# Reading the early pages' token lists ahead of the last scatters, with one flag and one branch at the end

## The chip, the cores and the metric

The kernel runs on one NeuronCore of a Trainium2 chip. The metric is the device time of one execution in microseconds (us), the median over several runs. The engines are named as in the profile: PE is TensorE (matrix products), DVE is VectorE, ACT is ScalarE, POOL is GpSimd, SP is SyncE, which here only issues DMA transfers and reads registers. The time before is 1185.52 us, the median of 3 runs (1181.2 to 1187.52).

## The reference

Three steps in float32, each on the output of the one before. The activations are 3072 tokens of 512 values in the second and third.

```python
# 1. banded attention, q, k, v: 4 x 8 x 768 x 64, window 128, 4 sinks
keep = (pos < n_sink) | ((rel >= 0) & (rel < window))
a = softmax(where(keep, scale * q @ k.T, -1e9))
x = (a @ v)                              # -> 3072 x 512
# 2. first MLP, 512 -> 2048 -> 512
h = x @ w_in;  x = (h - tanh(h)) @ w_out
# 3. routed MLP, 8 experts, top 1, 512 -> 1024 -> 512
logits = x @ w_gate + modality_bias[modality_id]
e_idx = argmax(logits);  probs = softmax(logits)
for e in range(8):
    mask = e_idx == e
    out[mask] = probs[mask, e] * (relu(x[mask] @ w1[e]) @ w2[e])
```

## The kernel before

**Chunks.** The tokens go through attention and the first MLP in 12 chunks of 256. The MLP of a chunk makes `h` (L175), three elementwise operations on DVE (`h` L189, `gy` L191) and ACT and POOL (`g`, L208 and L213), and the second product into `acc` (L245). Names carry the chunk: `gy11_4` belongs to chunk 11, the last. The chunk's result is stored in DRAM (`x2d`, L560), its router logits are computed (`lg`, L575), and `r_route` finds for each token its expert and its slot `sl` in a list of pages (L645). Two indirect scatters on POOL (L653) then write gate and token number to these slots in the DRAM tensor `xs`.

**Pages.** The slots are grouped into pages of 256, each of one expert. `r_order` puts the pages in the order in which they are computed, in the small tile `order`. Pages 0, 1 and 2 (`EARLY`) are chosen after chunk 10 among those that no token of chunk 11 can enter; the others are ordered after chunk 11 (names `ol...`). 13 pages are always computed (`NSTAT`); pages 13 to 18 stand in nested branches on the number of pages `npg` (L910 reads it, L915 branches), and behind them a branch on `redo` (L940, L941) leads to a general path for other masks. Neither is entered with these inputs.

**One page, and its names.** SP reads the expert from `order` (L718) and loads eight weight tiles `mr` of 512 KB each (L723). ACT casts each to `mh` (L731), DVE makes the remainder `ml` (L732): the split. SP reads the page number (L737) and loads the page's list `mpl` from `xs` (L740, 2 KB). DVE turns it into `mi` (L742) and `ms` (L744), and POOL gathers the rows of `x2d` by `ms` into two tiles `mx` (L750). PE transposes them (`mT`, L761), ACT and DVE make `mxt` (L764, L765). For each of 8 slices PE computes `mh` (12 matmuls, L775), ACT and DVE make `mg` (L778, L779), and PE adds six matmuls to `macc` (L792). At the end ACT scales by the gate (`mo`, L800) and POOL scatters the rows to `out` (L801). `mpl3` is page 3's list, `mg1_2` page 1's third slice.

**What sets the order.** Each step is filed with a time, as `add(time, function, ...)`; `emit` sorts by time and calls the functions, and a scheduler then orders each engine's queue within that. An engine takes its instructions strictly in that order: an instruction that waits holds all behind it. `m_events` files a page's steps; for the early pages no step comes before `first`, the time behind the early `r_order`. Weight tiles live in a pool of 33 buffers, gathered rows, page outputs and chunk outputs in a pool of 4, lists and their conversions in pools of 3.

Of the kernel before, what the change touches and what calls it, by code (L numbers as in the profile page):

```python
# [10 lines left out]
I32 = mybir.dt.int32  # L11
U8 = mybir.dt.uint8
AF = mybir.ActivationFunctionType
ALU = mybir.AluOpType
PSUM = bass.MemoryType.PSUM

P = 128
# [10 lines left out]
PG = 256  # L28
NPG = NT // PG + NE - 1
PADID = 4096.0  # L30
EARLY = 3
NSTAT = NT // PG + 1
# [8 lines left out]
class Kern:  # L41
# [658 lines left out]
    def r_redo(self, ok):  # L700

        nc = self.nc
        cp = self.cp
        mx, bad = cp.tile([P, 1], F32, name="ovmx"), cp.tile([P, 1], BF16, name="ovbad")
        nc.vector.tensor_reduce(out=mx, in_=self.over, axis=mybir.AxisListType.X, op=ALU.max)
        nc.vector.tensor_scalar(out=bad, in0=mx, scalar1=0.0, scalar2=None, op0=ALU.is_gt)
        ps = self.ps("x", F32, "ovps")
        nc.tensor.matmul(ps[:, :1], self.ones, bad, start=True, stop=True)
        t = cp.tile([P, 1], F32, name="ovt")
        nc.vector.tensor_scalar(out=t, in0=ps[:, :1], scalar1=0.0, scalar2=None, op0=ALU.is_equal)  # L710
        redo = cp.tile([P, 1], I32, name="redo")
        nc.vector.tensor_mul(t, t, ok)
        nc.vector.tensor_scalar(out=redo, in0=t, scalar1=-1.0, scalar2=1.0, op0=ALU.mult, op1=ALU.add)
        self.redo = redo


    def m_expert(self, g):
# [14 lines left out]
        nc.vector.tensor_sub(lo, r, f32(hi))  # L732
        self.mw[g, f] = (hi, lo)

    def m_xload(self, g):
        nc = self.nc
        pg = nc.sync.value_load(self.order[0:1, 0, g:g + 1], min_val=0, max_val=NPG - 1)  # L737
        n = PG // P
        pl = self.rp.tile([P, n, 2], F32, tag="mpl", name=f"mpl{g}", bufs=3)
        nc.sync.dma_start(pl, self.xs[bass.ds(pg * PG, PG), :].rearrange("(t p) w -> p t w", p=P))  # L740
        idx = self.rp.tile([P, n], I32, tag="mi", name=f"mi{g}", bufs=3)
        nc.vector.tensor_copy(idx, pl[:, :, 1])  # L742
        src = self.rp.tile([P, n], I32, tag="ms", name=f"ms{g}", bufs=3)
        nc.vector.scalar_tensor_tensor(out=src, in0=pl[:, :, 1], scalar=float(NT), in1=pl[:, :, 1],  # L744
                                       op0=ALU.is_lt, op1=ALU.mult)
        self.mx[g] = []
        rows = NT - CH if g < EARLY else NT
        for t in range(n):
            x = self.x2p.tile([P, DM], F32, tag="x2", name=f"mx{g}_{t}")
            nc.gpsimd.indirect_dma_start(out=x, out_offset=None, in_=self.x2d[:rows, :],  # L750
                                         in_offset=bass.IndirectOffsetOnAxis(ap=src[:, t:t + 1], axis=0))
            self.mx[g].append((x, idx[:, t:t + 1], pl[:, t, 0:1]))
# [54 lines left out]
    def m_events(self, add, g, t, t0=-1e9):  # L807
        n8 = FF // P
        o = self.o
        at = lambda d, fn, *a: add(max(t + d, t0), fn, *a)  # L810
        at(-o["me"], self.m_expert, g)
        at(-(o["mxe"] if g == 1 else o["mxl"]), self.m_xload, g)
        for j in range(PG // P):
            at(-o["mxt"] + 0.5 * j, self.m_xT, g, j)
            at(n8 + o["mlag"] - 0.5, self.m_out, g, j)
        for f in range(n8):
            at(f - o["mwl"], self.m_wload, g, f)
            at(f - o["mws"], self.m_wsplit, g, f)
            at(f, self.m_L1, g, f)
            at(f + o["mlag"], self.m_L2, g, f)  # L820
# [7 lines left out]
    def run_chunks(self, banded):  # L828
# [3 lines left out]
        with ExitStack() as st:  # L832
            pool = lambda n, b, **k: st.enter_context(tc.tile_pool(name=n, bufs=b, **k))
            self.yp = pool("y", self.o.get("y",2))
            self.xtp = pool("xt", self.o["bxt"])
            self.xpp = pool("xp", 1)
            if banded:
                self.rawp = pool("raw", self.o["raw"])
                self.spp = pool("sp", self.o["sp"])
                self.smp = pool("sm", self.o["bs"])  # L840
            self.gp = pool("g", self.o["bg"])
            self.psr = pool("psr", 6, space=PSUM)
            self.psa = pool("psa", 1, space=PSUM)
            self.x2p = pool("x2", self.o["x2"])
            self.rp = pool("rp", 1)
            self.X = None
            if banded:
                xs = pool("X", 1)
                self.X = xs.tile([P, 8, P], F32R, name="X")
                self.sT = [xs.tile([P, CH], F32R, name=f"sT{i}") for i in range(2)]  # L850
                for t in self.sT:
                    nc.gpsimd.memset(f32(t[2 * SK:]), 0.0)
            ev = []

            def add(t, fn, *a):
                ev.append((t, len(ev), fn, a))

            if banded:
                add(self.o["trc"], self.r_consts)
                add(self.o["trc"], self.r_reset)  # L860
            else:
                self.r_reset()
            add(self.o["tpf"], self.x_prefill, banded)
            for c in range(0 if banded else nch):
                add(16.0 * c - 2, self.x_load, c)
            for U in range(8 * nch if banded else 0):
                o = self.o
                t = 2.0 * U + o["u0"]
                add(t + o["tl"], self.a_load, U)
                add(t + o["tv"], self.a_loadv, U)  # L870
                if U >= o["nf"]:
                    add(t + o["ts"], self.a_split, U)
                    add(t + o["tsv"], self.a_splitv, U)
                for q in range(2):
                    add(t + o["tS"] + o["dS"] * q, self.a_S, U, q)
                    add(t + o["tN"] + o["dN"] * q, self.a_norm, U, q)
                    add(t + o["tT"] + o["dT"] * q, self.a_T, U, q)
                add(t + o["tPV"], self.a_PV, U)
            for f in range(NF):
                o = self.o  # L880
                add(f * o["wls"] + o["wl"], self.w_load, f, "i")
                add(f * o["wls"] + o["wl"] + o["wo"], self.w_load, f, "o")
                add(f * o["wds"] + o["wd"], self.w_decode, f, "i")
                add(f * o["wds"] + o["wd"] + o["wo"], self.w_decode, f, "o")
            for c in range(nch):
                t = 16.0 * c
                for pr in range(4):
                    add(t + self.o['txs'], self.xsplit, c, pr)
                for f in range(NF):
                    add(t + f, self.L1, c, f)  # L890
                    if f % 2:
                        add(t + f + self.o['tg'], self.gact if banded else self.gact_any, c, f // 2)
                    add(t + f + self.o["lag"], self.L2, c, f)
                t2 = t + NF - 0.9 + self.o["lag"]
                for q in range(CH // P):
                    add(t2 + self.o["tre"], self.r_evac, c, q)
                    add(t2 + self.o['trl'], self.r_logits, c, q)
                add(t2 + self.o['trr'], self.r_route, c)
                if c == nch - 2:
                    add(t2 + self.o["trr"] + .3, self.r_order, False)  # L900
                    first = t2 + self.o["trr"] + .35
            add(t2 + self.o["trr"] + .3, self.r_order, True)
            if banded:
                add(t2 + self.o["trr"] + .6, self.r_redo, self.ok)
            self.eg, self.mw, self.mx, self.mxt, self.mg, self.macc = {}, {}, {}, {}, {}, {}
            for g in range(NSTAT):
                self.m_events(add, g, 16.0 * nch + self.o["mt0"] + FF // P * g,
                              first if g < EARLY else t2 + self.o["trr"] + .35)
            self.emit(ev)
            np_ = nc.values_load(self.npi[0:1, 0:1], min_val=0, max_val=NPG)  # L910

            def rest(g):
                if g == NPG:
                    return
                with tc.If(np_ > g):  # L915
                    ev.clear()
                    self.m_events(add, g, 0.0)
                    self.emit(ev)
                    rest(g + 1)

            rest(NSTAT)

def program(tc, a, o={}):
    nc = tc.nc
    K = Kern(tc, a)
    K.o.update(o)
    with ExitStack() as st:
# [9 lines left out]
            K.ok = K.scalars(cp)  # L937
            K.band_masks(cp, sp)
        K.run_chunks(True)
        redo = nc.values_load(K.redo[0:1, 0:1], min_val=0, max_val=1)  # L940
        with tc.If(redo == 1):  # L941
            K.general()
            K.run_chunks(False)


def layouts(inp):
# [55 lines left out]
```

## Time and profile before

| | |
|---|---|
| median of 3 runs (lowest, highest) | 1185.52 us (1181.2, 1187.52) |
| the profiled execution: time, span | 1184.34 us, 1182.6 us |
| PE busy | 1118.5 us, 95% of the span, 7171 matmuls |
| DVE, ACT, POOL busy | 860.0, 689.8, 636.3 us |
| mean granted clock of PE | 0.98 |

The table by stretches says when an engine worked; `PEclk` in it is the clock granted to PE, 1.00 being full speed. In a timeline row the first number is the start and the second how long the instruction (or, with xN, the group) took; the bracket is the idle time of the engine before it and what ended that. What POOL does at the end in its sequencer (loads of flags, branches, semaphores, the drain) is in no busy time; the rows by source line list it, `POOLq` being POOL's sequencer.

### The profile page before, as it was taken

What the parts mean: (1) busy time and instruction counts of PE and PEld (TensorE: products, weight loads), DVE (VectorE), ACT (ScalarE), POOL (GpSimd) and SP (SyncE); (2) the same over time, 40 slices, a digit from 0 to 9 for tenths busy, and PEclk for the clock granted to TensorE, in tenths of its full rate; (3) what the DMA queues carried; (4) which work ended last, traced back from release to release, by engine and by line L of the source; (5) the groups of instructions that cost most, each with busy time, mean ns of one, the idle gap of its engine ahead of it and who ended that gap; (6) DMA issues with size and microseconds to landing.
All of it is one profiled execution on the core that took longest, in us unless ns stands there. A gap on an engine that the chain in (4) does not pass through costs nothing. (4 is left out here: it accounts for less than half of the span.)

```text
span 1182.6 us, 22303 instructions
## 1 busy us (share of the span) xinstructions
PE 1118.5 (95%) x7171; PEld 984.5 (83%) x7171; DVE 860.0 (73%) x2227; ACT 689.8 (58%) x1643; POOL 636.3 (54%) x877
## 2 busy tenths in 40 slices
PE   7889989999999999999999999999889999999992
PEld 3346789998999999998999998998778899999992
DVE  6989878787887878797878888756757565666610
ACT  3345565766666666666776757654536555556620
POOL 4887766767676767676776767643223112111200
PEclk9989999999999999999999999999989999999997
DMA  6654222313132222222222322003629776777500
GB/s 203 211 181 145 69 71 61 91 50 98 55 83 61 66 81 68 86 63 74 68 86 62 92 52 85 27 24 107 267 79 353 219 221 220 243 215 215 162 18 6
DMA packets 75127, 137.14 MB, mean 116 GB/s; under 512 B 16241, under 2 KB 51313, under 8 KB 74993
## 3 DMA queue, kind: packets, MB, share of 16 engines
q1 hardware_dynamic: 70064, 122.40, 34.0%
q0 software_dynamic: 4928, 13.14, 3.1%
q8 instruction: 61, 1.00, 0.4%
q14 instruction: 74, 0.60, 0.2%
HBM read 122.86 MB, written 13.17 MB: 115 GB/s over the span
## 5 line engine op out<-in xcount | busy, mean ns | idle before, releaser
L175 PE MATMUL h<-xt,wi 128*128 128x256 f32 x2304 | 350.6, 291 | 6.0 <-DVE xt L210 3.0
L175 PEld LDWEIGHTS h<-xt,wi 128*128 128x128 f32 x2304 | 313.1, 193 | 30.1 <-DVE xt L210 5.8
L245 PE MATMUL acc<-wo,g 128*128 128x512 f32 x1152 | 313.6, 399 | 5.1 <-POOL g L213 3.5
L245 PEld LDWEIGHTS acc<-wo,g 128*128 128x128 f32 x1152 | 201.8, 189 | 38.2 <-POOL g L213 5.4
L732 DVE TENSOR_TENSOR ml<-mr,mh 128x1024 fp32r<-128x1024 f32 x104 | 129.8, 1257 | 52.8 <-ACT mh L731 51.0
L213 POOL TENSOR_TENSOR g<-gy,g 128x512 fp32r<-128x512 f32 x96 | 132.4, 1379 | 63.0 <-ACT g L208 60.3
L775 PE MATMUL mh<-mxt,mh 128*128 128x256 f32 x832 | 156.1, 284 | 0.9 <-ACT mxt L764 0.7
L792 PE MATMUL macc<-mh,mg 128*128 128x512 f32 x416 | 147.9, 401 | 4.4 <-DVE mg L779 4.3
L775 PEld LDWEIGHTS mh<-mxt,mh 128*128 128x128 f32 x832 | 136.9, 192 | 9.4 <-ACT mxt L764 0.9
L801 POOL DMA_INDIRECT out_dram<-mo,mi x26 | 29.3, 1128 | 196.7 <-ACT mo L800 192.5
L352 POOL TENSOR_SCALAR_AFFINE_SELECT X<-fl 128x512 fp32r<-128x512 f32 (+1 forms) x192 | 117.0, 633 | 30.7 <-DVE fl L382 22.0
L325 ACT ACTIVATE e<-e,nm 128x160 f32<-128x160 f32 x192 | 81.8, 426 | 87.6 <-DVE nm L323 71.1
L731 ACT CAST mh<-mr 128x1024 fp32r<-128x1024 f32 x104 | 108.2, 1051 | 38.6 <-PE macc L792 25.3
L775 PE MATMUL mh<-mxt,ml 128*128 128x256 f32 x416 | 117.6, 284 | 0.0
L190 ACT ACTIVATE u<-u,kt 128x512 f32<-128x512 f32 x96 | 69.5, 723 | 44.5 <-DVE h L189 23.3
L334 POOL TENSOR_SCALAR e<-e,sm 128x160 f32<-128x160 f32 x192 | 88.5, 472 | 9.7 <-DVE sm L329 8.0
L792 PEld LDWEIGHTS macc<-mh,mg 128*128 128x128 f32 x416 | 77.9, 190 | 18.1 <-DVE mg L779 5.3
L778 ACT ACTIVATE mg<-mh 128x256 fp32r<-128x256 f32 x104 | 40.1, 386 | 90.0 <-PE mh L775 85.9
L213 POOL TENSOR_TENSOR B<-q,A 128x256 fp32r<-128x256 f32 x82 | 71.5, 871 | 39.1 <-ACT A L208 38.2
L213 DVE TENSOR_TENSOR K<-k,K 64x448 fp32r<-64x448 f32 x82 | 85.1, 1038 | 2.7
L213 POOL TENSOR_TENSOR V<-v,V 128x256 fp32r<-128x256 f32 x82 | 65.0, 793 | 35.3 <-ACT V L208 35.2
L792 PE MATMUL macc<-ml,mg 128*128 128x512 f32 x208 | 82.4, 396 | 0.0
(211 smaller groups left out, 2200.2 us busy)
## 6 DMA issues: line engine op xcount, KB each, us to landing
mr<-in_moe_w_dram SPq DMA_DIRECT2D x104, 512.0 KB
k<-in_k_dram SPq DMA_DIRECT2D x82, 224.0 KB
v<-in_v_dram SPq DMA_DIRECT2D x96, 128.0 KB
q<-in_q_dram SPq DMA_DIRECT2D x82, 128.0 KB
rawi<-in_moe_w_in_dram SPq DMA_DIRECT2D x16, 512.0 KB
rawo<-in_moe_w_out_dram SPq DMA_DIRECT2D x16, 512.0 KB
x2d<-x SPq DMA_DIRECT2D x24, 256.0 KB
k<-in_k_dram SPq DMA_DIRECT2D x14, 112.0 KB
```

Source lines behind the costliest of these rows:

```text
L175: nc.tensor.matmul(h, w[:, wl, k * P:(k + 1) * P], x[:, xl, k], start=(n == 0), stop=(n == 11))
L190: nc.scalar.activation(u, u, AF.Relu, bias=self.kt, accum_out=self.over[:, n:n + 1])
L213: (self.nc.vector if eng == "v" else self.nc.gpsimd).tensor_tensor(out=out, in0=a, in1=b, op=ALU.subtract)
L245: nc.tensor.matmul(o, g[:, gl, q:q + P], w[:, wl], start=(f == 0 and n == 0), stop=(f == NF - 1 and n == 2))
L325: nc.scalar.activation(e, e, AF.Exp, bias=nm, scale=-1.0, accum_out=u["sm"][:, t:t + 1])
L334: self.nc.gpsimd.tensor_scalar(out=e, in0=e, scalar1=r, scalar2=1.0, op0=ALU.mult, op1=ALU.mult)
L352: self.nc.gpsimd.affine_select(out=out, in_=in_, pattern=[[0, n], [s, P]], base=0, channel_multiplier=-s, compare_op=ALU.is_gt if prev els ...
L731: nc.scalar.copy(hi, r)
L732: nc.vector.tensor_sub(lo, r, f32(hi))
L775: nc.tensor.matmul(h, w[:, k * P:(k + 1) * P], x[:, xl, k], start=(n == 0), stop=(n == 11))
L778: nc.scalar.activation(gt[:, 0], h, AF.Relu)
L792: nc.tensor.matmul(self.macc[g][t], gt[:, gl, t * P:(t + 1) * P], w[:, DM:], start=(f == 0 and n == 0), stop=(f == n8 - 1 and n == 2))
```

## The change

`m_xload` is cut in two. `m_list` reads the page number, loads the list and makes `mi` and `ms`; `m_xload` issues the gathers. For pages 0, 1 and 2 `m_list` is filed at `first`, so that all three lists are read there; for the others it is filed just ahead of the gathers, as before. `r_redo` has two more DVE operations on 128x1 tiles for a flag `more`, 0 where there are at most 13 pages and no general path is needed. The code of pages 13 to 18 moves into a function of its own. At the end there is one load and one branch on `more`; inside it stand the pages beyond 13 and the branch on `redo`. Line numbers grow by 3 from L718 on and by 8 from L750 on; the end of the program moves from L998 to L1028.

```diff
@@ -712,6 +712,9 @@
         nc.vector.tensor_mul(t, t, ok)
         nc.vector.tensor_scalar(out=redo, in0=t, scalar1=-1.0, scalar2=1.0, op0=ALU.mult, op1=ALU.add)
         self.redo = redo
+        nc.vector.scalar_tensor_tensor(out=t, in0=self.npg, scalar=float(NSTAT), in1=t, op0=ALU.is_le, op1=ALU.mult)
+        self.more = cp.tile([P, 1], I32, name="more")
+        nc.vector.tensor_scalar(out=self.more, in0=t, scalar1=-1.0, scalar2=1.0, op0=ALU.mult, op1=ALU.add)
 
 
     def m_expert(self, g):
@@ -732,7 +735,7 @@
         nc.vector.tensor_sub(lo, r, f32(hi))
         self.mw[g, f] = (hi, lo)
 
-    def m_xload(self, g):
+    def m_list(self, g):
         nc = self.nc
         pg = nc.sync.value_load(self.order[0:1, 0, g:g + 1], min_val=0, max_val=NPG - 1)
         n = PG // P
@@ -743,9 +746,14 @@
         src = self.rp.tile([P, n], I32, tag="ms", name=f"ms{g}", bufs=3)
         nc.vector.scalar_tensor_tensor(out=src, in0=pl[:, :, 1], scalar=float(NT), in1=pl[:, :, 1],
                                        op0=ALU.is_lt, op1=ALU.mult)
+        self.ml[g] = (pl, idx, src)
+
+    def m_xload(self, g):
+        nc = self.nc
+        pl, idx, src = self.ml[g]
         self.mx[g] = []
         rows = NT - CH if g < EARLY else NT
-        for t in range(n):
+        for t in range(PG // P):
             x = self.x2p.tile([P, DM], F32, tag="x2", name=f"mx{g}_{t}")
             nc.gpsimd.indirect_dma_start(out=x, out_offset=None, in_=self.x2d[:rows, :],
                                          in_offset=bass.IndirectOffsetOnAxis(ap=src[:, t:t + 1], axis=0))
@@ -809,7 +817,12 @@
         o = self.o
         at = lambda d, fn, *a: add(max(t + d, t0), fn, *a)
         at(-o["me"], self.m_expert, g)
-        at(-(o["mxe"] if g == 1 else o["mxl"]), self.m_xload, g)
+        x0 = o["mxe"] if g == 1 else o["mxl"]
+        if g < EARLY and t0 > 0:
+            add(t0, self.m_list, g)
+        else:
+            at(-x0 - .01, self.m_list, g)
+        at(-x0, self.m_xload, g)
         for j in range(PG // P):
             at(-o["mxt"] + 0.5 * j, self.m_xT, g, j)
             at(n8 + o["mlag"] - 0.5, self.m_out, g, j)
@@ -902,23 +915,36 @@
             add(t2 + self.o["trr"] + .3, self.r_order, True)
             if banded:
                 add(t2 + self.o["trr"] + .6, self.r_redo, self.ok)
-            self.eg, self.mw, self.mx, self.mxt, self.mg, self.macc = {}, {}, {}, {}, {}, {}
+            self.eg, self.ml, self.mw, self.mx, self.mxt, self.mg, self.macc = {}, {}, {}, {}, {}, {}, {}
             for g in range(NSTAT):
                 self.m_events(add, g, 16.0 * nch + self.o["mt0"] + FF // P * g,
                               first if g < EARLY else t2 + self.o["trr"] + .35)
             self.emit(ev)
+
+    def more_pages(self):
+
+        tc, nc = self.tc, self.nc
+        with ExitStack() as st:
+            pool = lambda n, b, **k: st.enter_context(tc.tile_pool(name=n, bufs=b, **k))
+            self.xtp = pool("xt", self.o["bxt"])
+            self.gp = pool("g", self.o["bg"])
+            self.psr = pool("psr", 6, space=PSUM)
+            self.psa = pool("psa", 1, space=PSUM)
+            self.x2p = pool("x2", self.o["x2"])
+            self.rp = pool("rp", 1)
             np_ = nc.values_load(self.npi[0:1, 0:1], min_val=0, max_val=NPG)
 
             def rest(g):
                 if g == NPG:
                     return
                 with tc.If(np_ > g):
-                    ev.clear()
-                    self.m_events(add, g, 0.0)
+                    ev = []
+                    self.m_events(lambda t, fn, *a: ev.append((t, len(ev), fn, a)), g, 0.0)
                     self.emit(ev)
                     rest(g + 1)
 
             rest(NSTAT)
+
 
 def program(tc, a, o={}):
     nc = tc.nc
@@ -937,10 +963,14 @@
             K.ok = K.scalars(cp)
             K.band_masks(cp, sp)
         K.run_chunks(True)
-        redo = nc.values_load(K.redo[0:1, 0:1], min_val=0, max_val=1)
-        with tc.If(redo == 1):
-            K.general()
-            K.run_chunks(False)
+        more = nc.values_load(K.more[0:1, 0:1], min_val=0, max_val=1)
+        with tc.If(more == 1):
+            K.more_pages()
+            redo = nc.values_load(K.redo[0:1, 0:1], min_val=0, max_val=1)
+            with tc.If(redo == 1):
+                K.general()
+                K.run_chunks(False)
+                K.more_pages()
 
 
 def layouts(inp):
```

On SP the order at the early pages was: two weight loads of page 0, list 0, five weight loads, list 1, eleven weight loads, the two stores of `x2d`, ten register loads that wait for the last `r_order`, list 2, the remaining weight loads of page 2, two of page 3, list 3. Now it is: list 0, one weight load, lists 1 and 2, eighteen weight loads up to `mr2_2`, the stores, four weight loads, the register loads with `mr2_7`, `mr3_0` and `mr3_1` among them, list 3.

DVE around page 0's list, in the middle of chunk 11 (`ml0_0` is the first split of page 0), before:

```order
L191 SCALAR_TENSOR_TENSOR gy11_4_11583<-gy11_4_11583,h11_8_11543 128x512
L189 TENSOR_TENSOR h11_10_11594<-u11_5_11642,h11_10_11594 128x512
L742 CAST mi0_11505<-mpl0_11503 128x2
L744 SCALAR_TENSOR_TENSOR ms0_11507<-mpl0_11503 128x2
L191 SCALAR_TENSOR_TENSOR gy11_5_11643<-gy11_5_11643,h11_10_11594 128x512
```

and now:

```order
L191 SCALAR_TENSOR_TENSOR gy11_4_11613<-gy11_4_11613,h11_8_11573 128x512
L745 CAST mi0_11495<-mpl0_11493 128x2
L747 SCALAR_TENSOR_TENSOR ms0_11497<-mpl0_11493 128x2
L745 CAST mi1_11512<-mpl1_11510 128x2
L747 SCALAR_TENSOR_TENSOR ms1_11514<-mpl1_11510 128x2
L745 CAST mi2_11527<-mpl2_11525 128x2
L747 SCALAR_TENSOR_TENSOR ms2_11529<-mpl2_11525 128x2
L189 TENSOR_TENSOR h11_10_11624<-u11_5_11672,h11_10_11624 128x512
L191 SCALAR_TENSOR_TENSOR gy11_5_11673<-gy11_5_11673,h11_10_11624 128x512
```

Three conversions stand there in place of one, and `h11_10` stands behind them.

DVE at the beginning of page 1, behind the last routing (`more` is the new flag), before:

```order
L765 TENSOR_TENSOR mxt1_12130<-mT1_1_12169,mxt1_12130 128x4x128
L742 CAST mi2_12189<-mpl2_12187 128x2
L744 SCALAR_TENSOR_TENSOR ms2_12191<-mpl2_12187 128x2
L732 TENSOR_TENSOR ml1_4_12232<-mr1_4_11884,mh1_4_12231 128x1024
L779 SCALAR_TENSOR_TENSOR mg1_0_12220<-mh1_0_12207,mg1_0_12220 128x256
L779 SCALAR_TENSOR_TENSOR mg1_1_12258<-mh1_1_12245,mg1_1_12258 128x256
L732 TENSOR_TENSOR ml1_5_12272<-mr1_5_11933,mh1_5_12271 128x1024
L732 TENSOR_TENSOR ml1_6_12300<-mr1_6_11984,mh1_6_12299 128x1024
L732 TENSOR_TENSOR ml1_7_12337<-mr1_7_12012,mh1_7_12336 128x1024
L779 SCALAR_TENSOR_TENSOR mg1_2_12288<-mh1_2_12275,mg1_2_12288 128x256
```

and now:

```order
L773 TENSOR_TENSOR mxt1_12145<-mT1_1_12187,mxt1_12145 128x4x128
L717 TENSOR_SCALAR more_12169<-ovt_12163 128x1
L735 TENSOR_TENSOR ml2_2_12432<-mr2_2_12226,mh2_2_12431 128x1024
L787 SCALAR_TENSOR_TENSOR mg1_0_12223<-mh1_0_12210,mg1_0_12223 128x256
L735 TENSOR_TENSOR ml2_3_12486<-mr2_3_12264,mh2_3_12485 128x1024
L787 SCALAR_TENSOR_TENSOR mg1_1_12261<-mh1_1_12248,mg1_1_12261 128x256
L735 TENSOR_TENSOR ml2_4_12514<-mr2_4_12294,mh2_4_12513 128x1024
L747 SCALAR_TENSOR_TENSOR ms3_12473<-mpl3_12469 128x2
L735 TENSOR_TENSOR ml2_5_12554<-mr2_5_12331,mh2_5_12553 128x1024
L787 SCALAR_TENSOR_TENSOR mg1_2_12291<-mh1_2_12278,mg1_2_12291 128x256
```

The conversion of list 2 and the splits of page 1 have left this place; splits of page 2 and the conversion of list 3 (`ms3`) stand in it.

POOL from chunk 11's fourth `g` to the last chunk's scatters, before:

```order
L213 TENSOR_TENSOR g11_3_11538<-gy11_3_11532,g11_3_11538 128x512
L213 TENSOR_TENSOR g11_4_11589<-gy11_4_11583,g11_4_11589 128x512
L750 DMA mx0_0_11509<-x2d_64,ms0_11507 128x512
L750 DMA mx0_1_11511<-x2d_64,ms0_11507 128x512
L213 TENSOR_TENSOR g11_5_11649<-gy11_5_11643,g11_5_11649 128x512
L750 DMA mx1_0_11692<-x2d_64,ms1_11690 128x512
L750 DMA mx1_1_11694<-x2d_64,ms1_11690 128x512
L213 TENSOR_TENSOR g11_6_11727<-gy11_6_11721,g11_6_11727 128x512
L213 TENSOR_TENSOR g11_7_11801<-gy11_7_11795,g11_7_11801 128x512
L653 DMA xs_63<-pl_336,sl11_12094 4864x2 x2
L750 DMA mx2_0_12193<-x2d_64,ms2_12191 128x512
L750 DMA mx2_1_12195<-x2d_64,ms2_12191 128x512
```

and now:

```order
L213 TENSOR_TENSOR g11_3_11568<-gy11_3_11562,g11_3_11568 128x512
L758 DMA mx0_0_11539<-x2d_64,ms0_11497 128x512
L758 DMA mx0_1_11541<-x2d_64,ms0_11497 128x512
L213 TENSOR_TENSOR g11_4_11619<-gy11_4_11613,g11_4_11619 128x512
L758 DMA mx1_0_11707<-x2d_64,ms1_11514 128x512
L758 DMA mx1_1_11709<-x2d_64,ms1_11514 128x512
L213 TENSOR_TENSOR g11_5_11679<-gy11_5_11673,g11_5_11679 128x512
L213 TENSOR_TENSOR g11_6_11742<-gy11_6_11736,g11_6_11742 128x512
L213 TENSOR_TENSOR g11_7_11816<-gy11_7_11810,g11_7_11816 128x512
L758 DMA mx2_0_12196<-x2d_64,ms2_11529 128x512
L758 DMA mx2_1_12198<-x2d_64,ms2_11529 128x512
L653 DMA xs_63<-pl_336,sl11_12109 4864x2 x2
```

Each pair of gathers stands one or two instructions further ahead, and page 2's pair ahead of the scatters.

## Rows read from the trace of the kernel before

**Rows 1.** First line of the page.
```profile
span 1182.6 us, 22303 instructions
```

**Rows 2.** Stretch, length, busy us (count) PE, PEld, DVE, ACT, POOL; PEclk, DMA, GB/s.
```profile
820.00:840.00 20.00, 14.62 (x82) 12.07 (x81) 15.88 (x19) 16.44 (x25) 8.20 (x6) 0.95 1.00 379
...
870.00:880.00 10.00, 5.57 (x36) 4.27 (x35) 2.17 (x8) 6.17 (x9) 2.02 (x2) 0.95 0.20 52
880.00:890.00 10.00, 7.88 (x38) 7.06 (x39) 8.28 (x11) 4.21 (x6) 5.61 (x4) 0.71 0.88 286
...
950.00:1100.00 150.00, 150.00 (x977) 136.78 (x976) 92.98 (x129) 86.77 (x130) 33.89 (x28) 1.00 0.72 225
```

**Rows 3.** Waits of PE from 820 to 940 us: total, times, longest.
```profile
PE macc L792 <- DVE mg L779: 4.3, 1, 4.3
PE acc L245 <- POOL g L213: 3.5, 2, 3.1
...
PE mT L761 <- DMA mx<-x2d,ms: 1.3, 1, 1.3
```

**Rows 4.** Timeline of PE: start, duration, instruction, idle time before.
```profile
838.51 3.44 PE L245 MATMUL acc<-wo,g 128*128 128x512 f32 x8 [3.12 <-POOL g L213]
...
861.32 0.40 PE L792 MATMUL macc<-mh,mg 128*128 128x512 f32 x1
...
862.71 0.40 PE L775 MATMUL mh<-mxt,mh 128*128 128x256 f32 x2
...
864.14 0.40 PE L792 MATMUL macc<-mh,mg 128*128 128x512 f32 x1
...
880.79 1.22 PE L792 MATMUL macc<-mh,mg 128*128 128x512 f32 x2 [4.32 <-DVE mg L779]
...
885.96 0.63 PE L792 MATMUL macc<-mh,mg 128*128 128x512 f32 x2
...
889.78 0.63 PE L761 MATMUL mT<-ident,mx 128*128 128x128 f32 x4 [1.33 <-DMA mx<-x2d,ms]
```

**Rows 5.** Timeline of DVE.
```profile
819.82 0.69 DVE L189 TENSOR_TENSOR h<-u,h 128x512 f32<-128x512 f32 x1 [3.21 <-ACT u L186]
824.12 0.17 DVE L742 CAST mi<-mpl 128x2 int32<-128x2 f32 x1 [3.61 <-DMA mpl<-xs]
...
879.03 0.17 DVE L742 CAST mi<-mpl 128x2 int32<-128x2 f32 x1 [6.56 <-DMA mpl<-xs]
...
880.32 0.75 DVE L779 SCALAR_TENSOR_TENSOR mg<-mh,mg 128x256 fp32r<-128x256 f32 x2
```

**Rows 6.** Timeline of SP: issues to its DMA queue.
```profile
816.69 2.61 SPq L723 DMA_DIRECT2D mr<-in_moe_w_dram  x2
819.50 0.39 SPq L740 DMA_DIRECT2D mpl<-xs  x1
...
876.14 0.40 SPq L740 DMA_DIRECT2D mpl<-xs  x1
876.79 8.29 SPq L723 DMA_DIRECT2D mr<-in_moe_w_dram  x8
```

**Rows 7.** Timeline of POOL at the last chunk's second scatter.
```profile
872.05 1.00 POOL L653 DMA_INDIRECT xs<-pl,sl  x1 [0.30 <-issue]
```

**Rows 8.** Lines 915, 941 and 998 (end): duration ns min/median/max, first and last start.
```profile
L915 POOLq EVENT_SEMAPHORE  x4: 17/43/4642, 1163.5 to 1168.3; - x4
...
L915 POOLq COMPARE_BRANCH  x1: 53/53/53, 1163.3 to 1163.3; - x1
...
L915 POOLq INC_SWDGE_SEM  x1: 1699/1699/1699, 1168.4 to 1168.4; - x1
...
L941 POOLq EVENT_SEMAPHORE  x6: 17/30/43, 1173.2 to 1173.7; - x6
...
L941 POOLq COMPARE_BRANCH  x1: 45/45/45, 1170.5 to 1170.5; - x1
...
L998 POOLq DRAIN  x3: 40/107/6287, 1175.5 to 1182.3; - x3
```

## Prediction

> **What bounds the kernel now.** I read the span first [rows 1], then the table by stretches [rows 2], then the waits of TensorE around the last chunk [rows 3], then TensorE, VectorE, the SyncE queue and GpSimd instruction by instruction there [rows 4 to 7], and last the lines of the two branches at the end [rows 8]. The span is 1182.6 us and the profiled run took 1184.34 us, so 1.74 us lie outside it. That run is 1.18 us below the median of 1185.52 us; I sum in its frame and carry the difference over at the end.
>
> TensorE is the bound. From 890 us on it hardly waits; in 950 to 1100 it is busy for 150.00 of 150.00 us at a granted clock of 1.00 [rows 2]. So whatever it gains before 890 us is still there at the end, as long as the weights keep pace: the DMA share is 0.72 in that stretch, so the queues have room. The hole that the reader is to see is 870 to 890: TensorE is busy for 5.57 and 7.88 us of ten each, and in the second the granted clock is 0.71, between the levels of 2.4 and 1.2 GHz. Two of the named waits lie in it: 4.3 us for VectorE's `mg`, 1.3 us for page 2's gathered rows [rows 3]. An earlier one, 3.1 of 3.5 us for GpSimd's `g`, belongs to the stretch in which page 0's and page 1's lists arrive.
>
> Why VectorE was late: it came to page 2's `mi`, waited 6.56 us for the list, and only then (879.03) could do `ms`, a weight split and the two `mg` at 880.32 for which TensorE stood still [rows 5]. `mg` itself was ready to run: its operand is page 1's, and has nothing to do with page 2's list. The list was late because SyncE issued it at 876.14 [rows 6], 4.1 us after the second of the last chunk's scatters was issued at 872.05 [rows 7]; it waits for that scatter to land.
>
> **Middle of the program: the list of page 2.** The change reads it over 50 us earlier, so VectorE's next instructions there are a weight split and `mg`, both ready.
> - The wait of 4.32 us ahead of 880.79 goes [rows 4].
> - The clock goes with it. The 18 matmuls from 880.79 to 885.96 took 5.17 us. The same 6 and 12 took 861.32 to 862.71 and 862.71 to 864.14, together 2.82 us, at full clock. So 2.35 us more.
> - The wait of 1.33 us at 889.78 for page 2's rows goes too, as the gathers stand ahead of the last scatters on GpSimd now and take the rows long before.
>
> Sum: 4.32 + 2.35 + 1.33 = 8.0 us. Next in line is page 3's list, which still has to wait for the last scatters: its `ms` now stands on VectorE ahead of page 1's third `mg`, and behind it there wait that `mg`, the splits of page 2 and then TensorE. With the list issued at about 876.2 and 2.9 us from issue to use (876.14 to 879.03), `ms` of page 3 runs at about 879.1; a split and an `mg` behind it take 1.2 and 0.4 us (879.03 to 880.32 held two small operations and a split; two `mg` took 0.75), to about 881. TensorE, let go at 876.5, has to do the last two matmuls of page 1's first `macc` and four transposes (some 1.0 us, the two by the group of six, the four by the 0.63 us of 889.78), a group of 12, six `macc` and another group of 12 before it needs that third `mg`: 1.0 + 1.43 + 1.39 + 1.43 = 5.3 us, at 881.8. The cover is thin, 0.6 to 0.8 us; I count nothing for it and make its loss a rival. Weight loads are no longer held behind ten register loads that wait for the last page order and behind the list: they leave as buffers come free, so the queue ahead of page 3's list is shorter. The gathers of page 2, now ahead of the last scatters on GpSimd, wait for a buffer that page 1's first transposes free; these stand on TensorE ahead of what VectorE needs for the scatters' slots to be final, so I count no cost.
>
> The flag's two extra VectorE operations are of the size of the list conversion `mi`, 0.17 us [rows 5]; four of page 1's splits and two of page 2's move forward, in among page 0's `mg` and the routing. I put 0.5 us on both, since VectorE's smaller work feeds TensorE there without much slack; bounds 0 and 1.5.
>
> **Beginning: three lists in a row.** Before, VectorE waited until 824.12 for page 0's list, issued at 819.50 behind two weight loads that began at 816.69 [rows 5, 6]: 4.6 us from issue to use. Now list 0 is issued in front, one weight load follows, then lists 1 and 2, the last at about 820 (the two loads took 2.6 us from 816.69, and one has been swapped for a list and two register loads). With 2.9 to 4.6 us from issue to use the third is there at 822.9 to 824.6. But `h`, which was done in its place at 819.82 in 0.69 us, now stands behind the three lists, so what follows, `gy`, comes 0.5 us earlier to 1.2 us later. Against that, both pairs of early gathers leave GpSimd before the next `g`, where before page 1's pair stood ahead of a `g` for which TensorE waited 3.12 us (838.51) and whose eight matmuls took 3.44 us [rows 4]. That stretch is then set by VectorE, which is busy for 15.88 of 20 us from 820 to 840 with the wait for the list among the rest [rows 2], so I expect most of the 3.1 to come back as other short waits. Bounds: 2.5 us gained (the wait without most of its return) and 2 us lost (1.2 and the clock). I take 0.4 us gained, near the middle.
>
> **End of the program: one guard for two.** GpSimd ends last. Before, its first branch falls to a block at line 915 that waits 4.64 us for the last scatter's landing and then runs a counter update of 1.70 us from 1168.4 to 1170.1; then come the load of the second flag (line 940), the second branch at 1170.5, a gap to 1173.2, six semaphores, a second update, and at 1175.5 the drain of 6.29 us with which the program ends [rows 8]. With one guard there is one such block. The drain can start at 1170.1 instead of 1175.5: 5.4 us gained.
>
> The gap of 2.7 us behind the second branch is code that has to be fetched; behind the first branch it was 0.2 us (1163.3 to 1163.5). The one branch left skips more code than either, so I count 2.7 us for it, but it lies under the 4.64 us in which GpSimd waits for the landing anyway. Without that cover it would take 2.7 back. The Trainium skill (Runtime: NRT & Kernel Launch, section Instruction fetch mechanics) says that a taken branch whose target lies outside the fetched window makes the engine fetch the target first. The 2.7 us of line 941 agree, the 0.2 us of line 915 do not; by that rule alone the change would save one such fetch, 2.7 us, where the rows give 5.4 for the whole second block. Bounds of the term: 0 (the drain ends when it did) and 6.
>
> **Sum.** 8.0 + 5.4 + 0.4 - 0.5 = 13.3 us; 1184.34 - 13.3 = 1171.0 us, and 1172.2 with the median's 1.18. I say 1172 us. A measurement of this kernel tells a change from none beyond about 0.5%, 5.9 us, so from 1179.6 down and 1191.4 up.
>
> **Rivals.**
> - *The wait moves to page 3's list.* If that list takes the 4.6 us seen behind weight loads and is issued a little later, `ms` of page 3 holds VectorE until 881 to 882 and TensorE stands for some 2 to 3 us, with the clock's 2.35 once more: 5.5 of the 8.0 us come back, 1177.7 us. For it: the thin cover above, and two new weight loads directly ahead of the list. Against it: the burst of eight weight loads of 876.79 is spread out. 14%.
> - *The end is not shorter.* The drain's 6.29 us may be work that ends at its own time (the scatters' or the code's), so that starting it earlier only makes it longer. The profile doesn't say what it waits for. Then the 5.4 are lost: 1177.6 us. For it: its last scatter landed at 1168.2, 13.6 us before the drain's end, which is against it rather. 12%.
> - *VectorE is blocked at the beginning* (slower). Lists 1 and 2 sit behind the first weight load, and VectorE now does nothing until all three are there: `h`, `gy`, the splits of page 0 and, through `gy` and `g`, TensorE. Beyond 824.6 each microsecond costs one, and by the ratio above (2.35 on 4.32) another half for the clock. The gains of 13.3 us are used up when the third list is 8.6 us later than that, 13 us from its issue, against 4.6 us as the longest read here. At 16 us it would be 1190 us. 4%. The Trainium skill (DMA: Bandwidth & Descriptors, section Queues, rings and completion order) says that on each DMA engine descriptors are taken in ring order, so a list waits for the weights in front of it. The 4.6 against 2.9 us agree; by it two more weight loads' worth would have to stand ahead for a loss, and only one does.
> - *The change does not act*: the flag comes out as 1 and the outer block is entered. No page beyond 13 ran before and no general path, and the flag is made of the same two values. It would be about 1172 + 6 for the nested guard, or 1178 us. 2%.
> - *More comes back*: the beginning gives its 2.5 us and VectorE's forward work removes short waits: 1167 us. 8%.
>
> The forecast itself has 60%, with its own range of 1168 to 1176 us. The whole range is 1165 to 1180.5: it takes in both rivals near 1178 and leaves out the loss and the far tail. Faster by over 0.5%: the forecast, the larger gain and four in five of the cases near 1178, 0.87. Within 0.5%: 0.08. Slower: 0.05, the third rival and what I have not seen.
>
> **What the profile after would show.** If right, TensorE has no wait over 1 us between 870 and 890 us less what was gained before, its clock there is at 1.00, and the stretch list of waits for `macc` from `mg` is empty or under 1 us; GpSimd has one block of semaphores, one counter update, and the drain begins within 1 us of that update's end, with the same 6.3 us. If the first rival holds, VectorE waits for `mpl` ahead of a split of page 2. If the second holds, the drain is 11 to 12 us long. If the third holds, VectorE waits for `mpl` before `h` at 820 to 836 and TensorE for `gy` or `g` right after. The forecast is wrong if the time is above 1180.5 us, or if TensorE shows new idle time behind 890 us, where I count on none.

## The result, and the profile after

The changed kernel takes 1170.14 us, the median of 4 runs (1167.70 to 1173.07), against 1186.26 us for the kernel before (4 runs, 1181.20 to 1187.52); the ratio is 0.9881, with a 95% interval of 0.9854 to 0.9909. Forecast were 1172 us and a ratio of 0.9888. Two later series of the same kernel beside others gave 0.9887 (0.9859 to 0.9916) and 0.9891 (0.9869 to 0.9913). The profiled execution took 1170.8 us with a span of 1169.1 us, 13.5 us less than the span before [rows 1].

The sum is right; its parts are not. I cut both spans at five events that both have: chunk 10's second scatter, page 1's last transposes (the `mT` behind the `ovps` matmul), TensorE's last group of matmuls, the last output scatter, the end.

| stretch, us | before | after | gained | forecast |
|---|---|---|---|---|
| start to chunk 10's second scatter (same code) | 811.82 | 810.24 | 1.6 | 0 |
| to page 1's last transposes (beginning) | 58.71 | 57.79 | 0.9 | 0.4 - 0.5 |
| to TensorE's last matmuls (middle) | 290.43 | 286.09 | 4.3 | 8.0 |
| to the last output scatter | 2.66 | 2.67 | 0.0 | 0 |
| to the end of the span | 18.98 | 12.31 | 6.7 | 5.4 |

The first row is nothing but the spread between executions: the code there is the same, and over all profiles of this study that event came between 809.9 and 815.6 us. The middle gave about half of what was forecast, the end some more.

The table by stretches (columns as in [rows 2]) shows that the hole has become smaller and has moved:

```profile
830.00:840.00 10.00, 7.05 (x22) 5.37 (x22) 9.43 (x11) 9.73 (x15) 1.79 (x1) 0.66 1.03 419
870.00:880.00 10.00, 9.97 (x69) 8.89 (x67) 4.48 (x6) 5.33 (x8) 4.24 (x4) 1.00 0.77 155
880.00:890.00 10.00, 7.27 (x36) 6.44 (x37) 6.40 (x10) 4.09 (x6) 3.29 (x2) 0.83 0.83 274
950.00:1100.00 150.00, 150.00 (x977) 136.97 (x976) 92.34 (x129) 86.09 (x127) 34.46 (x26) 1.00 0.71 230
```

870 to 880 is full now (9.97 against 5.57 us); 880 to 890 is not, 7.27 us at a clock of 0.83. From 890 us on TensorE's list of waits is empty, as the prediction counted on. Waits of TensorE from 800 to 940 us:

```profile
PE acc L245 <- ACT g L208: 2.9, 1, 2.9
PE macc L800 <- DVE mg L787: 2.8, 1, 2.8
PE mh L783 <- ACT mxt L772: 0.7, 1, 0.7
PE acc L245 <- POOL g L213: 0.4, 1, 0.4
```

The wait for `mg` is still there, 2.8 us where it was 4.3 [rows 3]; the wait for page 2's rows has gone, and TensorE waits 0.4 and not 3.5 us for GpSimd's `g`, but now 2.9 for ScalarE's `g` (1.4 before). In TensorE's timeline both waits have their slow stretch behind them:

```profile
833.54 5.66 PE L245 MATMUL acc<-wo,g 128*128 128x512 f32 x12 [2.95 <-ACT g L208]
...
868.03 0.60 PE L769 MATMUL mT<-ident,mx 128*128 128x128 f32 x4
...
882.73 0.74 PE L800 MATMUL macc<-mh,mg 128*128 128x512 f32 x2 [2.76 <-DVE mg L787]
...
887.62 0.44 PE L783 MATMUL mh<-mxt,mh 128*128 128x256 f32 x2
```

The 20 matmuls from 882.73 to 887.62 took 4.89 us; at the full-clock rate of [rows 4] these are 0.46 + 1.43 + 1.39 = 3.28, so 1.6 us more went with the clock. The 12 matmuls at 833.54 took 5.66 us, where 12 of the same at 842.27 took 2.91.

VectorE shows whom `mg` waited for:

```profile
817.45 0.17 DVE L745 CAST mi<-mpl 128x2 int32<-128x2 f32 x1 [2.40 <-DMA mpl<-xs]
...
820.28 1.29 DVE L745 CAST mi<-mpl 128x2 int32<-128x2 f32 x1 [2.60 <-issue]
...
822.20 0.17 DVE L745 CAST mi<-mpl 128x2 int32<-128x2 f32 x1 [0.57 <-DMA mpl<-xs]
...
822.35 0.69 DVE L189 TENSOR_TENSOR h<-u,h 128x512 f32<-128x512 f32 x1
...
875.59 1.23 DVE L735 TENSOR_TENSOR ml<-mr,mh 128x1024 fp32r<-128x1024 f32 x1 [0.68 <-PE macc L800]
880.98 0.16 DVE L747 SCALAR_TENSOR_TENSOR ms<-mpl 128x2 int32<-128x2 f32 x1 [4.17 <-DMA mpl<-xs]
...
882.26 0.42 DVE L787 SCALAR_TENSOR_TENSOR mg<-mh,mg 128x256 fp32r<-128x256 f32 x1
```

At the beginning the three lists come one after the other, the third at 822.20 (forecast 822.9 to 824.6 in a run that was 1.6 us later), and `h` behind them. Near 880 VectorE stands for 4.17 us at page 3's `ms`, and `mg` comes behind that and one split. This is the first rival. SyncE issued that list only at 878.43; the seven weight loads from 848.37 on, for which it had been blocked before, were out by then, the last two, of page 3, at 869.90 and 871.70:

```profile
817.60 1.56 SPq L743 DMA_DIRECT2D mpl<-xs  x2
...
848.37 23.66 SPq L726 DMA_DIRECT2D mr<-in_moe_w_dram  x7
878.43 0.38 SPq L743 DMA_DIRECT2D mpl<-xs  x1
```

and on GpSimd the slot scatters are followed at once by page 0's outputs:

```profile
865.24 1.08 POOL L758 DMA_INDIRECT mx<-x2d,ms  x1 [10.98 <-PE mT L769]
869.67 1.02 POOL L653 DMA_INDIRECT xs<-pl,sl  x1 [3.36 <-DVE sl L645]
870.99 1.00 POOL L653 DMA_INDIRECT xs<-pl,sl  x1 [0.30 <-issue]
872.30 1.16 POOL L809 DMA_INDIRECT out_dram<-mo,mi  x1 [0.31 <-ACT mg L786]
873.76 1.40 POOL L809 DMA_INDIRECT out_dram<-mo,mi  x1 [0.30 <-issue]
```

From the second scatter (870.99) to the list (878.43) it took 7.44 us; before it was 4.09 [rows 6, 7]. What SyncE waited for ahead of the list is the scatters' landing, for page 2's list before and for page 3's list now:

```profile
SPq L740 <- DMA xs<-pl,sl: 3.4, 1, 3.4
```

```profile
SPq L743 <- DMA xs<-pl,sl: 5.6, 1, 5.6
```

The end, by source line as in [rows 8]:

```profile
L967 POOLq EVENT_SEMAPHORE  x6: 17/30/647, 1159.1 to 1160.1; - x6
...
L967 POOLq COMPARE_BRANCH  x1: 53/53/53, 1156.4 to 1156.4; - x1
L967 POOLq INC_SWDGE_SEM  x1: 1708/1708/1708, 1160.2 to 1160.2; - x1
...
L1028 POOLq DRAIN  x3: 40/107/6287, 1162.0 to 1168.8; - x3
```

One block, one counter update from 1160.2 to 1161.9, and the drain right behind it at 1162.0, 6287 ns as before. The one branch's gap is 2.7 us (1156.4 to 1159.1) and lies under the landing of the last scatter, of which only 0.65 us is still waited for.

### The profile page after: what moved, and what is told of

It is laid out like the page before. It is cut to its first block, busy times and chain, and to the rows that moved or that the text cites. A ratio compares the mean times of both kernels' runs of the same rounds, so it can differ in the third digit from the quotient of the medians.

```text
span 1169.1 us, 22281 instructions
## 1 busy us (share of the span) xinstructions
PE 1117.7 (96%) x7171; PEld 985.3 (84%) x7171; DVE 859.1 (73%) x2229; ACT 690.0 (59%) x1643; POOL 636.8 (54%) x877
## 4 chain that ended last, share of the span: by engine, by line
PE 74%; DVE 10%; issue 6%; POOL 4%; DMA 3%; ACT 1%; SPq 1%; POOLq 0%; DVEq 0%; ACTq 0%
PE h L175 20%; PE acc L245 19%; PE mh L783 11%; PE macc L800 10%; PE s L311 2%; PE R L414 2%; PE lg L575 2%; PE s L312 2%; PE T L344 1%; PE T L345 1%; DVE K L213 1%; PE R L416 1%; PE xT L568 1%; DVE yo L146 1%; PE R L410 1%
```

## Experiments

Is the end worth 5 to 7 us by itself, and the lists the rest? **tail_only** has the one guard and reads the lists in the old places:

```diff
-        if g < EARLY and t0 > 0:
-            add(t0, self.m_list, g)
-        else:
-            at(-x0 - .01, self.m_list, g)
-        at(-x0, self.m_xload, g)
+        def both(g):
+            self.m_list(g)
+            self.m_xload(g)
+        at(-x0, both, g)
```

> The one flag and one branch at the end, with all lists read where they were before. Theory (one whole block of flag load, branch and counter update goes): GpSimd has one counter update and its drain of 6.3 us begins right behind it; from the start of GpSimd's last scatter to the end of the span 12.3 to 13.6 us against 19.0 before; the time is 5.4 to 6.7 us lower, ratio about 0.995. Middle unchanged: VectorE still waits over 6 us for page 2's list and TensorE over 4 us for mg. Rival (the end was shorter only because the last scatter happened to land 1.3 us sooner after its issue, and the drain stretches): 0 to 1.3 us, drain 11 us.

Measured: 1176.94 us, ratio 0.9939 (0.9920 to 0.9959), 12.94 us from the last scatter to the end. Its GpSimd has one update, and the same drain right behind it:

```profile
L966 POOLq EVENT_SEMAPHORE  x6: 17/30/1034, 1169.9 to 1171.3; - x6
...
L966 POOLq INC_SWDGE_SEM  x1: 1708/1708/1708, 1171.4 to 1171.4; - x1
...
L1027 POOLq DRAIN  x3: 40/107/6287, 1173.1 to 1180.0; - x3
```

The stretch from page 1's transposes on is 291.45 us, where the kernel before had 290.43. VectorE waited 5.9 us for page 2's list and TensorE 3.7 us for `mg`, slightly under the 6 and 4 us that I expected. So the end alone is worth some 6 us (18.98 - 12.94 = 6.0 in the profiles, 1183.47 - 1176.94 = 6.5 between the medians of that series), and the drain is a fixed 6.29 us that moves with its start: the second rival falls.

**lists_only** has the lists of the changed kernel and the end of the kernel before:

```diff
...
-        at(-(o["mxe"] if g == 1 else o["mxl"]), self.m_xload, g)
+        x0 = o["mxe"] if g == 1 else o["mxl"]
+        if g < EARLY and t0 > 0:
+            add(t0, self.m_list, g)
+        else:
+            at(-x0 - .01, self.m_list, g)
+        at(-x0, self.m_xload, g)
...
```

> The early lists as in the changed kernel, with the two guards of before at the end and no flag. Theory (the wait moved: page 3's list now holds VectorE): VectorE waits about 4 us for page 3's list, TensorE about 2.8 us for mg and then runs slow for some 5 us; end of the program 19.0 us from the last scatter as before; the time is about 5 us lower than before, ratio 0.9955. Rival (the prediction's sum, page 2's wait simply goes): no wait of TensorE over 1 us between 870 and 890 us, about 8 us lower, ratio 0.993.

Measured: 1175.92 us, ratio 0.9935 (0.9913 to 0.9958): some 7.5 us, where I had expected about 5. The end takes 18.61 us and the middle 283.08. The wait moved here too, but it was shorter in this execution:

```profile
PE macc L797 <- DVE mg L784: 1.4, 1, 1.4
...
879.26 0.16 DVE L744 SCALAR_TENSOR_TENSOR ms<-mpl 128x2 int32<-128x2 f32 x1 [3.20 <-DMA mpl<-xs]
```

0.9939 times 0.9935 is 0.9875; the whole change gave 0.9881. The two parts add up.

What is the wait for page 3's list worth? **conv_pool** leaves the conversions of pages 0 to 2 on VectorE and makes the others on GpSimd, right ahead of the gathers that need them (`ms` in three small operations there):

```diff
+        e = nc.vector if g < EARLY else nc.gpsimd
...
-        nc.vector.tensor_copy(idx, pl[:, :, 1])
+        e.tensor_copy(idx, pl[:, :, 1])
...
+            e.tensor_scalar(out=ok, in0=pl[:, :, 1], scalar1=float(NT), scalar2=None, op0=ALU.is_lt)
+            e.tensor_tensor(out=ok, in0=pl[:, :, 1], in1=ok, op=ALU.mult)
+            e.tensor_copy(src, ok)
...
```

> The changed kernel, with the two conversions of the lists of pages 3 and up on GpSimd, right ahead of the gathers that use them, so that no list is waited for on VectorE behind page 2. Theory (page 3's list on VectorE costs TensorE 2.76 us of waiting and 1.6 us of slow clock, 4.89 us from 882.73 to 887.62 against 3.28 for the same 20 matmuls at full clock): both go, 4.4 us below the changed kernel, about 1166 us, ratio to before 0.984 to 0.985; TensorE has no wait for mg over 0.5 us from 860 to 900 us. Rival (TensorE would next wait for something else, page 2's weights or splits): no gain against the changed kernel, 1170 us, with another wait of 2 us or more in that place.

Measured: 1166.48 us, ratio 0.9863 (0.9834 to 0.9892), and no wait for `mg`; the middle stretch is 281.20 us against 286.09. As the intervals of this and of the changed kernel overlapped, both were run again in one series, **after_third** (the changed kernel unaltered) and **conv_again** (this one unaltered):

> The changed kernel a third time, beside the next one on the same chip: about 1170.5 us, ratio to before about 0.988; from page 1's last transposes to TensorE's last matmuls 283 to 287 us, depending on when page 3's list comes.

> The kernel with the conversions from page 3 on on GpSimd once more. If TensorE's wait for page 3's list is really gone with it: 281 to 282 us in that stretch again, no wait for mg, and a median 3 to 5 us below the changed kernel of the same call. If its first median was luck: the same median as the changed kernel within 1 us.

Measured: 1172.73 us, 0.9891 (0.9869 to 0.9913) and 1165.95 us, 0.9845 (0.9826 to 0.9865). The intervals no longer meet, and each of conv_again's five runs (1165.45 to 1167.34 us) is below all six of after_third (1168.13 to 1176.54); the middle is 285.54 against 281.20 us. So the wait for page 3's list on VectorE is what the middle lost. conv_again's waits of TensorE from 815 to 930 us, and its table by stretches:

```profile
PE acc L245 <- ACT g L208: 3.7, 1, 3.7
PE acc L245 <- POOL g L213: 0.9, 1, 0.9
PE mh L790 <- ACT mxt L779: 0.7, 1, 0.7
```

```profile
870.00:880.00 10.00, 9.88 (x70) 9.30 (x71) 6.87 (x13) 7.24 (x12) 4.56 (x4) 1.00 0.63 133
880.00:890.00 10.00, 10.00 (x65) 9.01 (x64) 6.41 (x8) 5.30 (x8) 3.83 (x6) 1.00 0.87 273
```

GpSimd waits instead, and no wait of TensorE in the list above follows from it:

```profile
882.09 0.23 POOL L753 TENSOR_SCALAR mk<-mpl 128x2 f32<-128x2 f32 x1 [6.13 <-DMA mpl<-xs]
...
884.49 1.06 POOL L765 DMA_INDIRECT mx<-x2d,ms  x1 [0.64 <-PE macc L807]
```

Why did page 3's list come late? Ahead of it on SyncE are two weight loads of page 3 that the change set free; behind the scatters on GpSimd are page 0's outputs, which page 2's gathers no longer hold. **weights_held** puts the two loads behind the list:

```diff
...
+        with self.tc.issue_after(self.li.ins):
+            self.m_wload(g, f)
...
+            if g == EARLY and f < 2 and t0 > 0:
+                at(-x0, self.m_wheld, g, f)
```

> The changed kernel, with page 3's first two weight loads issued by SyncE behind page 3's list and not ahead of it. In the changed kernel the list is issued 7.4 us after the second of the last scatters is issued, before it was 4.1 us. Theory (the 1 MB of weights issued at 869.9 and 871.7 runs beside the scatters and makes them land late): 4 to 5 us again, VectorE's wait for the list under 2 us, TensorE's wait for mg under 1 us, 2.5 to 4 us below the changed kernel. Rival (page 0's two output scatters, which now follow on GpSimd directly behind the slot scatters, make them land late): still about 7 us from scatter to list, and the time of the changed kernel within 1 us.

Measured: 1172.56 us, ratio 0.9908 (0.9875 to 0.9941), not faster than the changed kernel, with 2.0 us of TensorE's waiting for `mg` where I expected under 1, though the list follows the second scatter by 4.09 us again (875.28 to 879.37). The order changed elsewhere with it: page 0's outputs stood ahead of the slot scatters, and the second scatter was issued at 875.28 and not 870.99, 2.9 us later if the 1.4 us by which this execution was behind at chunk 10's scatters are taken off. So the scatters began later by nearly what they landed sooner, and two suspects had been moved at once. Two runs part them. **weights_held2** keeps the outputs behind the scatters too:

```diff
+        with self.tc.issue_after(self.slots) if g == 0 and self.slots else ExitStack():
             i = nc.gpsimd.indirect_dma_start(out=self.a["out"][:, :], ...
```

> The changed kernel with page 3's first two weight loads behind page 3's list on SyncE, and page 0's output scatters kept behind the slot scatters on GpSimd, as they stand in the changed kernel. Theory (weights running beside them make the scatters land late): the list is issued about 4.1 us after the second scatter, as before the change and as in the run before this, in which the outputs stood ahead of the scatters. Rival (the outputs that follow directly make them land late): 6.8 to 7.5 us, as in the changed kernel.

Measured (one execution, 1168.55 us): 5.18 us, between the theory's 4.1 and the rival's 6.8. **outs_held** is conv_pool with page 0's outputs held behind the first conversion of list 3:

```diff
...
+        with self.tc.issue_after(self.cv.ins):
+            self.m_scat(g, t)
...
+            if g == EARLY and t0 > 0 and self.late:
+                for j in range(PG // P):
+                    at(-x0 - .005, self.m_scat_late, 0, j)
```

> The changed kernel with the conversions of the lists from page 3 on on GpSimd, and page 0's two output scatters held on GpSimd until page 3's list is there; the two weight loads stay ahead of the list. Theory (weights): the list is still issued 6.8 to 7.5 us after the second scatter. Rival (outputs): about 4.1 us.

Measured (one execution, 1168.18 us): 7.27 us. The rows of outs_held, second scatter, weight loads and list:

```profile
872.15 1.00 POOL L653 DMA_INDIRECT xs<-pl,sl  x1 [0.30 <-issue]
```

```profile
871.06 2.08 SPq L726 DMA_DIRECT2D mr<-in_moe_w_dram  x2
879.42 0.38 SPq L743 DMA_DIRECT2D mpl<-xs  x1
```

and of weights_held2:

```profile
871.97 1.00 POOL L653 DMA_INDIRECT xs<-pl,sl  x1 [0.30 <-issue]
```

```profile
877.15 0.38 SPq L747 DMA_DIRECT2D mpl<-xs  x1
```

So the weights account for most of it: 7.27 us with them and without the outputs, 5.18 with the outputs and without them, 4.09 and 3.76 with neither (the kernel before, tail_only), and 6.84 to 9.53 with both, in six profiles. These are single executions, and those with both spread by 2.7 us: no profile with the two loads within 2 us of the second scatter is under 6.84 and none without them over 5.2, but the 1.1 us between 4.09 and 5.18 can't be put down to the outputs.

**after_again** is the changed kernel unaltered; **conv_all** moves the conversions of pages 0 to 2 to GpSimd as well:

```diff
-        e = nc.vector if g < EARLY else nc.gpsimd
+        e = nc.gpsimd
...
```

> The changed kernel once more, beside the next one on the same chip. Expected: about 1170 us, ratio to before 0.987 to 0.989; page 3's list issued 6.8 to 7.5 us after the second of the last scatters; TensorE waits 1.4 to 2.8 us for mg there.

> The changed kernel with the conversions of all lists on GpSimd, those of pages 0 to 2 as well, so that VectorE waits for no list at the beginning either. In the changed kernel VectorE idles 2.4, 2.6 and 0.6 us for the three lists and ScalarE 4.1 us behind it. Theory (this delays chunk 11's chain and page 0's splits, and TensorE's 2.95 us wait at 833.5 with its slow clock follows from it): from chunk 10's second scatter to page 1's last transposes 55 to 56 us against 57.8, and with the 4.4 us of the run before, 5.5 to 7 us below the changed kernel, 1164 us. Rival (ScalarE's weight casts set that stretch, whatever VectorE waits for): 57 us or more, about 1166 us, as with the conversions from page 3 on alone. Second rival (small GpSimd operations delay g there): slower than that, 1168 us.

Measured: after_again 1171.15 us, 0.9887 (0.9859 to 0.9916), and a list that came later than in any other run, 9.53 us after the scatter, with 4.2 us of waiting for `mg`, outside what I expected. conv_all 1168.39 us, 0.9870 (0.9842 to 0.9899), no better than conv_pool (0.9863 and 0.9845). VectorE's waits for the lists at the beginning are gone, and the slow stretch with them (granted clock 1.00 from 830 to 840 us), but the way from chunk 10's scatter to page 1's transposes is 56.80 us, where conv_pool and conv_again had 56.84 and 58.42. That lies between the theory's 55 to 56 us and the rival's 57 or more; the time is that of the second rival, 1168 us, but no run shows whether for its reason. TensorE's one wait of 2.5 and 3.7 us there for ScalarE's `g` has become several short ones:

```profile
PE acc L245 <- POOL g L213: 2.2, 3, 1.3
PE mh L786 <- DVE gy L191: 0.8, 1, 0.8
...
```

In conv_all page 0's outputs stood ahead of the slot scatters, and page 3's two weight loads were issued 4.0 and 2.7 us before the second scatter and not beside it; the list followed that scatter by 5.19 us.

## Why the prediction came out

**Middle: the mechanism was right, its size was not.** Page 2's list did hold VectorE, and reading it early took away the 4.32 and the 1.33 us. The term fell short in its sentence that the cover of 0.6 to 0.8 us for page 3's list would hold, for which I counted nothing. Measured from page 1's last transposes, page 3's `ms` came after 880.98 - 868.03 = 12.95 us, where the prediction had 879.1 - 870.53 = 8.6. Of the 4.4 us between them 3.35 are the later landing (7.44 for 4.09), and 1.4 the scatters' later place behind these transposes (870.99 - 868.03 = 2.96 us, before 872.05 - 870.53 = 1.52); the way from issue to use was 0.3 shorter. The 8.0 us shrank to 4.3 here, and to 3.2, 4.9 and 7.4 in after_again, after_third and lists_only, which read the lists in the same order; it is whole again, 9.2 us, where VectorE doesn't wait for list 3 (290.43 - 281.20), less 0.5 us by which the last output scatter comes later there (3.17 us behind the last matmuls, before 2.66).

**The step that failed by name** is "so the queue ahead of page 3's list is shorter". It was, for the list itself, which took 2.55 us from issue to use. I had not asked what the freed weight loads do to the scatters that the list waits for. In the kernel before, SyncE was blocked there and the DMA share was 0.01 up to 870 us, so the scatters were issued to idle queues:

```profile
860.00:870.00 10.00, 10.00 (x70) 8.64 (x68) 6.88 (x42) 1.86 (x5) 0.00 (x0) 1.00 0.01 2
```

The Trainium skill (DMA: Bandwidth & Descriptors, section Queues, rings and completion order) says that a transfer's semaphore increment lands only after every earlier write of the same DMA engine, across its queues; the 7.27 us of outs_held against 4.09 agree, but no run here tells that order from a mere sharing of the DMA engines. I had weighed another rule of that section, order within one ring, and at the beginning of the program, where it cost nothing: the third list came within the bounds.

**First rival: it held, at some 3 to 5 us instead of 5.5.** It was the better account of the middle, and I gave it 14%. That the profile's total was right all the same, 13.5 against 13.3 us, is partly luck: the 3.7 us that the middle lacks are made up by 1.3 us more at the end, 1.0 at the beginning and 1.6 of spread ahead of the change. The medians fell by 16.1 us here and by 11.9 and 11.3 in the two later series. The chance of 0.87 for a faster kernel is also lower than its own terms, which add up to 0.60 + 0.08 + 0.8 * 0.28 = 0.90.

**End: right.** 5.4 us come from the block that went. The other 1.3 us are the last output scatter, which was waited for until 4.54 and 4.14 us behind its issue with two guards (before, lists_only) and until 3.1 to 3.9 with one, in the seven profiles that waited for it. Why it is sooner there was not tried and stays open. The branch's 2.7 us were covered as forecast in the changed kernel; in conv_again, conv_all and outs_held the gap behind the branch was 3.0 to 3.4 us and no landing was waited for any more, so there it stands in the end's 12.0 to 12.4 us. That the one branch left has such a gap agrees with the Trainium skill's rule on taken branches (Runtime: NRT & Kernel Launch, section Instruction fetch mechanics), by which the engine must fetch a target outside its window first.

**Beginning: within its bounds, and too small to tell.** The stretch took 58.71 before and 57.79, 57.88 and 58.33 in the three profiles of the changed kernel, but 57.90 in tail_only, whose order there is that of before. What I expected in kind did happen: the 3.12 us for GpSimd's `g` went and came back as 2.95 us for ScalarE's. What the flag's two operations cost can't be told: lists_only, without them, took 57.64 us. The third rival, VectorE blocked there for long, did not happen: the third list was used 3.4 us after its issue. That rival's last sentence also asks for too little: by its own rows two weight loads ahead cost a list 1.7 us (4.6 against 2.9), and a loss needed 8.6.

## What to carry to other kernels

When an early load frees an engine that waited at a semaphore, look at every queue that this engine or its feeder had been holding back: what it now releases will run beside the next transfer that others wait for, and can make that one late. A conversion that waits for a late transfer is better placed on the engine that uses it, ahead of the use, than in the queue of one that feeds the bound: that gave 4 us and more for page 3's list, and nothing further for the early lists, whose waits were short. And two guards in a row at the end of a program, each taken seldom, cost a whole block each on the engine that ends last; one flag for both is cheap.

## What the runs showed that I had not expected

A small write can wait for bulk loads on another queue: the last slot scatters, of 128 slots with 8 bytes each, let the list go 3.8 to 4.1 us after the second one's issue in quiet queues and only after 6.8 to 9.5 us with 1 MB of weight loads beside them (5.2 us in the two runs between these cases, weights_held2 and conv_all). The drain at the end took 6.29 us in all twelve profiles, whatever stood ahead of it. And the twelve profiles of this study, of kernels whose code is the same up to chunk 10's scatters, reached them between 809.9 and 815.6 us, eight of them within 1 us of 811; a part worth 1 us can't be read from one profile's span, but from its own stretch it can.
